# A spectral filter and a mixture of experts in one kernel: the second batch's transform takes one product instead of two from its sixth step on

## The chip, the cores and the metric

The kernel runs on one core of one Trainium2 chip. A core has five engines that work at the same time and wait for each other by semaphores: PE (TensorE, matrix products; its weight loads are listed as PEld), DVE (VectorE), ACT (ScalarE), POOL (GpSimd) and SP (SyncE, which here issues most transfers). Each works through its own list of instructions strictly in order. The metric is the device time of one execution in microseconds (us).

## The reference

Eight batches of 2496 tokens with 256 channels are filtered along the tokens by a Fourier transform, and each filtered token then goes through one of eight experts, the one that its own routing logits choose:

```python
X = np.fft.rfft(x, axis=1)
F = (filt_r + 1j * filt_i)[None, :, :]
y = np.fft.irfft(X * F, n=x.shape[1], axis=1)      # per batch
...
logits = xn @ en.T / tau                            # xn, en: rows of unit length
expert_idx = np.argmax(logits, axis=1)
probs = softmax(logits)                             # written out in the reference
for e in range(E):
    h = np.maximum(x[mask] @ w1[e], 0.0)
    out[mask] = gate_w[mask, None] * (h @ w2[e])
```

In the second half `x` is the filtered signal, `gate_w` the probability of the chosen expert, and `mask` the tokens that chose expert `e`.

## The kernel before

**The filter.** 2496 is 64 times 39, so the transform of a batch is done in two directions: along b (39 long) and along a (64 long). Each batch is a group `g`, 0 to 7, and goes through three parts. `conv_s1` (L448) transforms along b and writes to DRAM (`SD`). `conv_s2` (L469) reads that back in ten steps, and in each step transforms along a, multiplies by the filter and transforms back along a, and writes to DRAM (`ZD`). `conv_sb` (L562) reads `ZD`, transforms back along b (tiles `y`), makes the rows of the tokens, their logits and their place in the list of their expert, and POOL scatters the rows to DRAM (`XS`) by indirect DMAs.

**One step of `conv_s2`.** PE makes `s2` (shown as `s_g_k`: group, step; `conv_s1`'s tiles `s1` are shown in the same form) from the input `a` and the constant c2: the upper 64 partitions hold the real parts, the lower 64 the imaginary ones. A complex product by the filter needs the spectrum times the real part of the filter (`yy`, DVE, L497) and the spectrum with its halves swapped times the imaginary part (`xs`, DVE, L499, with the sign `sgn`). There are two ways to join them. In groups 0 and 1 (`g < FOLDED`) the halves are not swapped: `xs` is taken from `s2` as it is, and PE makes two products into one tile `sa`, `yy` with m1 and `xs` with m2, whose halves stand swapped (L555). In later groups ACT copies the halves of `s2` crosswise into `xs` (L528, L529), DVE multiplies in place, POOL adds `xs` to `yy` (L536; for the first three steps of the third batch DVE does), and PE makes one product. Two steps later (`SAL`) `sa` of step k follows, ACT copies it to `z` (L558), and a DMA on SP's queue writes it to `ZD`.

**The precision of these products.** In groups 0 to 2 the products of L439 and L555 have f32 operands; a 128x512 product of that kind appears in the trace as two matmul instructions. Products of L444 take three passes over rounded parts.

**The experts.** Tokens are worked off in slots, 128 or 256 rows of one expert (`Slot`, L899). A slot reads its rows from `XS` (`xT`), and for each quarter of F PE makes `ph` (up, L967), ACT and DVE make `h`, and PE makes `po` (down, L992) two quarters later. ACT copies the result to `o` (L1006), and POOL scatters it to the output (L1007). The first eight slots have a fixed expert and 128 rows each (tiles `ph_4_0` and the like, with `xTf`); then come the slots of group 0, and so on, so that the names `ph_0_0` start again with each group.

**The order of the work.** Slots of one group and the filter of the next are interleaved: `spread` takes steps of `later(g)` between the quarters of the slots at a pace worked out from the number of steps and of slots, and where the queue of slots is empty it first takes the next group's filter to its end. The first part of the program, up to the first steps of the fixed slots, stands on PE, ACT, DVE and SP in the order of the code (`manual_schedule`); from there on a scheduler orders the instructions of each engine by its own estimate of when they are ready. So an edit can move other instructions too.

**Buffers.** `s2` and `sa` share two PSUM buffers (`ps_c`), `yy` and `xs` six buffers of SBUF (`hl`, `XYB`), and the inputs `a` and the next batch's `in` four (`INB`).

## Time and profile before

| | us |
|---|---|
| median of three runs (lowest to highest) | 1345.94 (1344.21 to 1347.41) |
| the profiled execution | 1342.77 |
| its span, first to last instruction | 1340.7 |
| PE busy | 1247.3 |
| DVE busy | 941.0 |
| ACT busy | 761.6 |
| POOL busy | 486.0 |

The profile is of one execution. The busy time of an engine says how much it has to do, not what it waits for; the chain of waits follows the work that ended last back from releaser to releaser, and the timelines show, in brackets, how long an engine stood idle before an instruction and what ended that. Times in the rows are from the start of the span. The stretch that the change touches directly, the second batch's `conv_s2` from its sixth step on, lies at about 196 to 225 us. The granted clock (PEclk) is a share of PE's full speed: 1.00 is 2.4 GHz, and stretches at 1.2 GHz lower the mean of a window.

### The profile page before, as it was taken

What the parts mean: (1) busy time and instruction counts of PE and PEld (TensorE: products, weight loads), DVE (VectorE), ACT (ScalarE), POOL (GpSimd) and SP (SyncE); (2) the same over time, 40 slices, a digit from 0 to 9 for tenths busy, and PEclk for the clock granted to TensorE, in tenths of its full rate; (3) what the DMA queues carried; (4) which work ended last, traced back from release to release, by engine and by line L of the source; (5) the groups of instructions that cost most, each with busy time, mean ns of one, the idle gap of its engine ahead of it and who ended that gap; (6) DMA issues with size and microseconds to landing.
All of it is one profiled execution on the core that took longest, in us unless ns stands there. A gap on an engine that the chain in (4) does not pass through costs nothing.

```text
span 1340.7 us, 36475 instructions
## 1 busy us (share of the span) xinstructions
PE 1247.3 (93%) x11027; PEld 979.1 (73%) x11027; DVE 941.0 (70%) x3081; ACT 761.6 (57%) x1760; POOL 486.0 (36%) x566
## 2 busy tenths in 40 slices
PE   7966799978998989999999999999998999999997
PEld 2343586645676768787888788878887888889887
DVE  1446696775688668877888788868785885444664
ACT  2165465845655676668666775778565842333343
POOL 0003312174156325542565256424632165111221
PEclk8988899979999989999999999999999999999999
DMA  7799967988878787769779977787774554221211
GB/s 222 268 310 347 258 186 206 215 244 239 193 187 224 211 182 175 221 191 217 159 196 235 192 191 204 219 186 186 172 205 127 119 119 103 58 49 41 57 42 41
DMA packets 272354, 241.27 MB, mean 180 GB/s; under 512 B 167123, under 2 KB 212182, under 8 KB 270373
## 3 DMA queue, kind: packets, MB, share of 16 engines
q1 hardware_dynamic: 243965, 177.87, 53.0%
q0 software_dynamic: 24320, 57.97, 14.4%
q10 hardware_dynamic: 3880, 3.03, 0.8%
q8 instruction: 104, 1.70, 0.5%
q14 instruction: 85, 0.70, 0.2%
HBM read 122.32 MB, written 85.57 MB: 155 GB/s over the span
## 4 chain that ended last, share of the span: by engine, by line
PE 71%; DMA 17%; DVE 5%; issue 3%; ACT 2%; SPq 1%; POOL 1%; DVEq 0%; ACTq 0%; POOLq 0%
PE ph L967 26%; PE po L992 26%; PE s L444 5%; DMA yT<-rows 4%; DMA f<-ZD 4%; PE s L439 3%; DMA f<-in_filt 3%; PE y L444 3%; PE sa L444 2%; DMA SD<-s 2%; PE sa L555 2%; PE y L439 2%; DMA XS<-rows,ixi 1%; PE tp L593 1%; PE lp L610 1%
## 5 line engine op out<-in xcount | busy, mean ns | idle before, releaser
L992 PE MATMUL po<-W,h 128*128 (+1 forms) x3824 | 494.0, 273 | 0.3 <-DVE h L976 0.3
L967 PE MATMUL ph<-xT,wp 128*128 128x256 f16 (+2 forms) x4224 | 472.3, 258 | 9.0 <-DMA xT<-XS 3.9
L967 PEld LDWEIGHTS <-wp 128*128 128x128 f16 x4224 | 358.0, 98 | 85.8 <-issue 37.0
L992 PEld LDWEIGHTS <-h 128*128 128x128 f16 x3824 | 360.9, 98 | 69.7 <-issue 25.9
L975 ACT ACTIVATE h<-ph 128x512 f16<-128x512 f32 (+2 forms) x384 | 202.0, 527 | 246.8 <-PE ph L967 194.1
L1007 POOL DMA_INDIRECT out_dram<-o,meta x153 | 158.7, 1037 | 330.7 <-ACT o L1006 250.6
L976 DVE SCALAR_TENSOR_TENSOR h<-ph,h 128x512 f16<-128x512 f32 (+2 forms) x384 | 227.4, 592 | 46.0 <-ACT h L975 44.1
L951 DVE COPY wp<-W 128x1024 f16 x352 | 166.4, 473 | 120.2 <-PE ph L967 117.0
L790 POOL DMA_INDIRECT XS<-rows,ixi x176 | 179.9, 1022 | 128.6 <-issue 97.1
L536 POOL TENSOR_TENSOR yy<-yy,xs 128x512 f32<-128x512 f32 x57 | 77.6, 1364 | 98.9 <-DVE xs L499 72.3
L497 DVE TENSOR_TENSOR yy<-s,f 128x256 f32<-128x256 f32 x160 | 61.5, 417 | 56.3 <-DMA f<-in_filt 22.9
L400 POOL DMA_DIRECT2D in<-in_x x66 | 38.9, 590 | 160.5 <-DVE xp L413 53.9
L635 DVE SCALAR_TENSOR_TENSOR rows<-y,rr,rows 128x256 f16<-128x256 f32 x176 | 76.7, 477 | 23.6 <-ACT rows L632 22.1
L668 ACT ACTIVATE rows<-y 128x256 f16<-128x256 f32 x176 | 67.1, 396 | 28.8 <-PE y L439 27.4
L632 ACT ACTIVATE rows<-y,rr 128x256 f16<-128x256 f32 x176 | 75.4, 493 | 10.3 <-DVE rr L673 8.3
L1006 ACT ACTIVATE o<-po,meta 128x256 f32<-128x256 f32 x148 | 64.0, 479 | 28.9 <-PE po L992 27.5
L558 ACT COPY z<-sa 128x512 f32<-128x512 f32 x80 | 46.7, 584 | 43.9 <-PE sa L555 37.6
L465 ACT COPY s<-s 128x512 f32<-128x512 f32 x88 | 52.4, 596 | 26.3 <-PE s L439 17.7
L412 ACT CAST yp<-yy 128x512 fp32r<-128x512 f32 x50 | 31.0, 619 | 62.3 <-POOL yy L536 62.0
L595 ACT COPY yT<-tp 128x512 f16<-128x512 f16 x99 | 58.5, 604 | 12.8 <-PE tp L593 8.4
L444 PE MATMUL s<-xp,c1h 117*128 117x512 f32 (+1 forms) x144 | 61.3, 432 | 0.0
L499 DVE SCALAR_TENSOR_TENSOR xs<-xs,sgn_sb,f 128x256 f32<-128x256 f32 x120 | 58.8, 529 | 0.0
(209 smaller groups left out, 1659.1 us busy)
## 6 DMA issues: line engine op xcount, KB each, us to landing
f<-in_filt SPq DMA_DIRECT2D x160, 256.0 KB
a<-SD SPq DMA_DIRECT2D x80, 256.0 KB
ZD<-z SPq DMA_DIRECT2D x80, 256.0 KB
f<-ZD SPq DMA_DIRECT2D x80, 240.0 KB
SD<-s SPq DMA_DIRECT2D x70, 240.0 KB
in<-in_x POOLq DMA_DIRECT2D x66, 234.0 KB
W<-in_w SPq DMA_DIRECT2D x14, 1024.0 KB
in<-in_x SPq DMA_DIRECT2D x22, 234.0 KB
```

What stands on the lines that cost most here:

```text
L444: nc.tensor.matmul(out_, w[:k], b, start=(n == 0), stop=(n == 2))
L536: (nc.vector if g == 2 and k < 3 else nc.gpsimd).tensor_tensor(out=yy, in0=yy, in1=xs, op=ALU.add)
L632: nc.scalar.activation(rows[:, i, 0:D], y[:, i], AF.Copy, scale=rr[:, u:u + 1])
L635: nc.vector.scalar_tensor_tensor(out=rows[:, i, D:2 * D], in0=y[:, i], scalar=rr[:, u:u + 1], in1=rows[:, i, 0:D], op0=ALU.mult, op1=ALU.s ...
L668: nc.scalar.activation(rows[:, i, D:2 * D], y[:, i], AF.Square, accum_out=ssq[:, u + i:u + i + 1])
L790: i = nc.gpsimd.indirect_dma_start(out=XS, out_offset=bass.IndirectOffsetOnAxis(ap=ix, axis=0), in_=src, in_offset=None)
L951: last["dve"] = nc.vector.tensor_copy(wp, src)
L967: last["pe"] = nc.tensor.matmul(ph[:, fi, :size], wp[:, k * 2 + wh, fi * P:(fi + 1) * P], xT[:, xh * 2 + k, :size], start=(c == 0), stop=( ...
L975: last["act"] = nc.scalar.activation(h[:, 0, :, :size], ph[:, :, :size], AF.Relu)
L976: last["lo"] = nc.vector.scalar_tensor_tensor(out=h[:, 1, :, :size], in0=ph[:, :, :size], scalar=0.0, in1=h[:, 0, :, :size], op0=ALU.max, ...
L992: nc.tensor.matmul(self.po[:, s], h, self.Wp[:, off + wh * 1024:off + wh * 1024 + D], start=(fp == 0 and fi == 0 and c == 0), stop=(fp == ...
L1007: i = nc.gpsimd.indirect_dma_start(out=out, out_offset=bass.IndirectOffsetOnAxis(ap=self.meta[:n, s, 0:1].bitcast(I32), axis=0), in_=o, in ...
```

## The change

`FOLDED` no longer counts groups but steps of group 1: group 0 takes two products as before, groups 2 to 7 one as before, and group 1 two up to its fifth step and one from its sixth on (k = 5 to 9).

```diff
--- before.py
+++ after.py
@@ -62,7 +62,7 @@
 WARM = {-1: 8, 12: 26, 35: 22, 40: 6}
 FRONT = 0
 FIXED = 128
-FOLDED = 2
+FOLDED = 5
 PT = 1
 
 
@@ -515,6 +515,7 @@
         for k in range(NK + lag):
             if k + INB - 1 < NK:
                 ain[k + INB - 1] = load_a(k + INB - 1)
+            swap = g > 1 or g == 1 and k >= FOLDED
             if k < NK:
                 pt = ps_c.tile([P, 2, D], F32, tag="c", name=f"s2_{g}_{k}")
                 if g >= G_S2:
@@ -524,15 +525,15 @@
                 product(pt.rearrange("p j c -> p (j c)"), cons["c2"], ain.pop(k))
 
                 xs = cw.tile([P, 2, D], F32, tag="hl", bufs=XYB, name=f"xs{g}_{k}")
-                if g >= FOLDED:
+                if swap:
                     nc.scalar.copy(xs[0:NA], pt[NA:P])
                     nc.scalar.copy(xs[NA:P], pt[0:NA])
                 fts = fin.pop(k)
                 yy = cw.tile([P, 2, D], F32, tag="hl", bufs=XYB, name=f"yy{g}_{k}")
                 filtered(yy, pt, fts, 0)
-                filtered(xs, xs if g >= FOLDED else pt, fts, 1)
+                filtered(xs, xs if swap else pt, fts, 1)
                 ys[k] = [yy]
-                if g >= FOLDED:
+                if swap:
                     (nc.vector if g == 2 and k < 3 else nc.gpsimd).tensor_tensor(out=yy, in0=yy, in1=xs, op=ALU.add)
                 else:
```

For each of these five steps there are two more ACT copies and one POOL addition, and one product less; the DVE multiplication of `xs` reads `xs` where it read `s2`. From L515 on, lines stand one further down in the changed kernel.

The order of other instructions changes as well, from the second batch's sixth step to the third batch's end; on each engine it is the same again from the first steps of the fourth batch's `conv_s2` on. Three places follow; "..." stands for rows left out, most of them repeats with their weight loads.

On PE, at the last two steps of the second batch's `conv_s2` (`sa_8`, `sa_9`), among the last fixed slots (`ph_7`, `po_6`, `po_7`); `s_2_0` is the first product of the third batch's `conv_s1`. Before:

```order
L555 MATMUL sa_8_2450<-yy_8_2394,m_sb 128x512
L555 MATMUL sa_8_2450<-xs_8_2393,m_sb 128x512
L932 TENSOR_LOAD tb_2017
...
L967 MATMUL ph_7_1_2793<-xTf_2074,W 128x128
...
L992 MATMUL po_6_2638<-W,h_6_3_2675 128x256
...
L555 MATMUL sa_9_2474<-yy_9_2432,m_sb 128x512
L555 MATMUL sa_9_2474<-xs_9_2431,m_sb 128x512
...
L967 MATMUL ph_7_2_2910<-xTf_2074,W 128x128
```

And now:

```order
L556 MATMUL sa_8_2462<-yy_8_2404,m_sb 128x512
...
L968 MATMUL ph_7_2_2920<-xTf_2074,W 128x128
...
L993 MATMUL po_7_2951<-W,h_7_0_2746 128x256
...
L993 MATMUL po_7_2951<-W,h_7_1_2847 128x256
...
L968 MATMUL ph_7_3_2990<-xTf_2074,W 128x128
...
L993 MATMUL po_7_2951<-W,h_7_2_2933 128x256
L556 MATMUL sa_9_2485<-yy_9_2444,m_sb 128x512
L444 MATMUL s_2_0_2579<-xp_0_0_2575,c1h 128x512
L444 MATMUL s_2_0_2579<-xp_0_0_2575,c1l 128x512
L444 MATMUL s_2_0_2579<-xp_0_1_2576,c1h 128x512
```

`sa_9` now has the slot products `ph_7_2`, `ph_7_3` and 13 of `po_7` ahead of it, and the product of `xs` is gone.

On POOL, first around the additions of the last two steps, then where the second batch's rows are scattered (L790 before, L791 now; `o_3` is the result of group 0's fourth slot). Before:

```order
L400 DMA in_3_2563<-in_x 117x512
L400 DMA in_4_2625<-in_x 117x512
L400 DMA in_5_2680<-in_x 117x512
L400 DMA in_6_2739<-in_x 117x512
L1007 DMA out_dram<-o_6_0_2874,metaf_2075 19968x256
...
L1007 DMA out_dram<-o_2_0_4135,meta_2_3584 19968x256
L790 DMA XS<-rows_4_2784,ixi_4_3487 161920x258 x2
L790 DMA XS<-rows_5_2887,ixi_4_3487 161920x258 x2
L790 DMA XS<-rows_6_2956,ixi_4_3487 161920x258 x2
L790 DMA XS<-rows_7_3042,ixi_4_3487 161920x258 x2
L1007 DMA out_dram<-o_3_0_4337,meta_3_3835 19968x256
L790 DMA XS<-rows_8_3153,ixi_8_3665 161920x258 x2
```

And now:

```order
L400 DMA in_3_2573<-in_x 117x512
L537 TENSOR_TENSOR yy_8_2404<-yy_8_2404,xs_8_2401 128x512
L1008 DMA out_dram<-o_6_0_2884,metaf_2075 19968x256
L537 TENSOR_TENSOR yy_9_2444<-yy_9_2444,xs_9_2441 128x512
L400 DMA in_4_2635<-in_x 117x512
...
L1008 DMA out_dram<-o_2_0_4145,meta_2_3594 19968x256
L1008 DMA out_dram<-o_3_0_4347,meta_3_3845 19968x256
L791 DMA XS<-rows_4_2794,ixi_4_3497 161920x258 x2
L791 DMA XS<-rows_5_2897,ixi_4_3497 161920x258 x2
L791 DMA XS<-rows_6_2966,ixi_4_3497 161920x258 x2
L791 DMA XS<-rows_7_3052,ixi_4_3497 161920x258 x2
L791 DMA XS<-rows_8_3163,ixi_8_3675 161920x258 x2
```

The addition for `yy_9` stands behind the output of `o_6`, and the output of `o_3` has moved from between the second and third block of scatters to in front of the second.

On PE, where the second batch's first slot (`ph_0_0`) comes among the steps of the third batch's `conv_s2` (`s_2_k` from `a_k`, `sa_k`). Before:

```order
L555 MATMUL sa_2_4025<-yy_2_3947,m_sb 128x512
L439 MATMUL s_2_5_4038<-a_5_3940,c_sb 128x512
L555 MATMUL sa_3_4053<-yy_3_3975,m_sb 128x512
L439 MATMUL s_2_6_4109<-a_6_3968,c_sb 128x512
L555 MATMUL sa_4_4124<-yy_4_4015,m_sb 128x512
...
L967 MATMUL ph_0_0_4249<-xT_0_4096,wp_0_0_4213 128x256
...
L967 MATMUL ph_0_1_4278<-xT_0_4096,wp_0_1_4247 128x256
...
L439 MATMUL s_2_7_4140<-a_7_4008,c_sb 128x512
...
L555 MATMUL sa_5_4155<-yy_5_4043,m_sb 128x512
```

And now:

```order
L439 MATMUL s_2_5_4048<-a_5_3950,c_sb 128x512
L556 MATMUL sa_3_4063<-yy_3_3985,m_sb 128x512
...
L968 MATMUL ph_0_0_4259<-xT_0_4106,wp_0_0_4223 128x256
...
L968 MATMUL ph_0_1_4288<-xT_0_4106,wp_0_1_4257 128x256
...
L439 MATMUL s_2_6_4119<-a_6_3978,c_sb 128x512
...
L556 MATMUL sa_4_4134<-yy_4_4025,m_sb 128x512
```

The slot's first products stand in front of `s_2_6` and `sa_4` instead of behind them.

## Rows read from the trace of the kernel before

**Rows 1.** The page: the span, and PE's busy time, share and instructions.

```profile
span 1340.7 us, 36475 instructions
...
PE 1247.3 (93%) x11027; PEld 979.1 (73%) x11027; DVE 941.0 (70%) x3081; ACT 761.6 (57%) x1760; POOL 486.0 (36%) x566
```

**Rows 2.** Busy time by windows: us, each engine (instructions), PE clock, DMA.

```profile
core 0: us, PE busy (x) PEld busy (x) DVE busy (x) ACT busy (x) POOL busy (x), PEclk, DMA share, GB/s
200.00:210.00 10.00, 10.00 (x70) 6.06 (x69) 8.41 (x27) 4.58 (x10) 2.83 (x3) 1.00 0.71 205
210.00:220.00 10.00, 10.00 (x80) 6.69 (x78) 9.51 (x22) 6.54 (x15) 2.24 (x3) 1.00 0.62 222
...
340.00:350.00 10.00, 8.38 (x46) 5.40 (x47) 4.41 (x13) 4.76 (x16) 0.00 (x0) 0.83 0.90 176
...
370.00:380.00 10.00, 10.00 (x97) 7.61 (x95) 8.93 (x47) 8.62 (x27) 6.17 (x7) 1.00 0.84 198
```

**Rows 3.** The chain of waits, 194 to 240 us: start, us, what.

```profile
205.34 0.67 PE ph L967 x12
...
222.58 1.72 PE sa L555 x4
...
228.77 6.66 DMA f<-ZD
```

**Rows 4.** PE's timeline: start us, us, instruction, count, idle before it and its releaser.

```profile
223.28 1.02 PE L555 MATMUL sa<-xs,m_sb 128*128 128x512 f32 x2
...
233.17 1.13 PE L439 MATMUL y<-f,csb_sb 120*128 120x512 f32 x2 [1.70 <-DMA f<-ZD]
...
308.90 2.34 PE L967 MATMUL ph<-xT,wp 128*128 128x256 f16 x20 [2.43 <-DMA xT<-XS]
...
341.62 1.93 PE L439 MATMUL y<-f,csb_sb 120*128 120x512 f32 x2 [3.28 <-DMA f<-ZD]
...
419.31 2.25 PE L967 MATMUL ph<-xT,wp 128*128 128x256 f16 x19 [1.46 <-DMA xT<-XS]
```

**Rows 5.** The chain of waits, 280 to 345 us.

```profile
299.65 5.90 DMA XS<-rows,ixi
...
319.26 1.31 PE ph L967 x12
...
330.54 0.59 ACT z L558
...
331.15 2.84 DMA ZD<-z
...
334.13 7.45 DMA f<-ZD
```

**Rows 6.** Groups by line: engine, operation, count, ns shortest/median/longest, first and last start.

```profile
L528 ACT COPY xs<-s x60: 582/582/587, 283.8 to 1017.2; 64x512 f32<-64x512 f32 x60
...
L529 ACT COPY xs<-s x60: 577/577/581, 284.4 to 1017.8; 64x512 f32<-64x512 f32 x60
...
L536 POOL TENSOR_TENSOR yy<-yy,xs x57: 1260/1293/1916, 300.6 to 1020.1; 128x512 f32<-128x512 f32 x57
```

**Rows 7.** DVE's timeline, 295 to 330 us.

```profile
300.57 1.94 DVE L499 SCALAR_TENSOR_TENSOR xs<-xs,sgn_sb,f 128x256 f32<-128x256 f32 x2
...
305.14 0.87 DVE L499 SCALAR_TENSOR_TENSOR xs<-xs,sgn_sb,f 128x256 f32<-128x256 f32 x2
...
326.17 1.76 DVE L413 TENSOR_TENSOR xp<-in,xp 117x512 fp32r<-117x512 f32 x1
...
328.52 0.67 DVE L413 TENSOR_TENSOR xp<-in,xp 117x512 fp32r<-117x512 f32 x1
```

**Rows 8.** POOL's timeline, 285 to 330 us.

```profile
291.37 1.16 POOL L1007 DMA_INDIRECT out_dram<-o,meta  x1 [0.30 <-issue]
292.84 1.28 POOL L790 DMA_INDIRECT XS<-rows,ixi  x1 [0.30 <-DVE us L864]
...
300.56 1.26 POOL L536 TENSOR_TENSOR yy<-yy,xs 128x512 f32<-128x512 f32 x1
...
326.09 1.29 POOL L536 TENSOR_TENSOR yy<-yy,xs 128x512 f32<-128x512 f32 x1 [2.00 <-DVE xs L499]
```

## The prediction

> **What bounds the kernel now.** I read the page first: TensorE (PE) is busy 93% of the span [rows 1], so any PE instruction taken away looks like time gained. Then the windows, for the stretch in which the second batch goes through its transform along a. From 200 to 220 us PE is busy 20 of 20 us at full granted clock, and VectorE (DVE) 8.41 and 9.51 of 10 [rows 2]: PE is full and DVE nearly so. Then the chain of waits. To the last product of the transform the chain is PE without a gap; right behind it stands a transfer of 6.66 us, the read of f from ZD [rows 3]. On PE's timeline the last product issues from 223.28 and is over at about 224.1 (0.86 later); the first product that needs that transfer, y_0 of the second batch, starts at 233.17 after 1.70 us of idle PE [rows 4]. So the stretch has two clocks: PE's work in its written order, and the path of the batch: sa_9, copy, write to ZD, read back, y. PE waits for the path, not the path for PE.
>
> The same picture comes twice more. The second batch's rows are scattered from POOL one after the other, the last at 299.65; its landing, 5.90 us, holds the read of the first slot [rows 5], and PE takes that slot up at 308.90 after 2.43 us of idling [rows 4]. And in the third batch the copy behind its last product starts at 330.54, the write takes 2.84 and the read 7.45 us [rows 5], and PE stands idle for 3.28 us before y_0 at 341.62 [rows 4].
>
> **What goes.** Five products of xs with m2. A pair of products (yy and xs) takes 1.72 us on PE [rows 3], one of them 0.86, so 5 x 0.86 = 4.3 us leave PE while it is full. DVE keeps its four multiplications a step; the one for xs reads SBUF instead of PSUM.
>
> **What comes.** Ten ACT copies of 0.58 us and five POOL adds of 1.26 to 1.9, median 1.29 [rows 6]. ACT gets 5.8 us in 25; it lies beside PE. For the last step it is a path: copies 0.58 + 0.58, xs on DVE 0.87 [rows 7], add 1.26 [rows 8], 3.3 us in sum. In front of yy_9's add POOL has the DMA of o_6 (second order excerpt), 1.16 us and 0.30 of issue for such a one [rows 8]: 4.8 us. Between s_1_9 and sa_9 PE has by the new order 36 products of 128 columns, 19 of 256 and two of the f32 kind (sa_7, sa_8): at 0.67 and 1.31 us per 12 [rows 3, 5] that is 2.0 + 2.1 + 1.7 = 5.8 us. The cover is 1.0 us, and one queueing of DVE behind an add uses it up. I take 0.3 us late; the ends are 0 and 3.3 (the second rival).
>
> **What moves.** The order is rebuilt from 195 us until the third batch is through; from the fourth batch's transform on it is the same as before. So a shift at that point goes to the end unchanged, and I follow the path to there.
>
> 1. sa_9 of the second batch. Ahead of it now stand 24 slot products of 128 columns and 16 of 256 that stood behind it (first excerpt): 1.3 + 1.7 = 3.1 us. Of the 4.3 us, 1.2 are left to the path; less 0.3 for the add, 0.9.
> 2. y_0 of the second batch. Between sa_9 and it the order has 8 products of 128 columns and 11 of 256 fewer, 0.4 + 1.2 us; with the 1.2 of point 1 PE's work ahead of it falls by 2.8 to 2.9, while its data comes 0.9 earlier: the idle time of 1.70 becomes about 3.7. After an idle time of 3.28 the next pair took 1.93 us at a granted clock of 0.83, after 1.70 it took 1.13 [rows 2, 4]; for that I charge 0.5 of the 0.8. Path: 0.4 us earlier.
> 3. The scatter. The DMA of o_3, 1.16 us and its issue of 0.30 between the second and third block of scatters [rows 8], now stands in front of the second block (second excerpt), where POOL waits for the indices anyway. Path: 1.9 us earlier, first slot at about 307.0.
> 4. The third batch's transform. Before, s_2_6 and sa_4 stood ahead of the first slot; now behind (third excerpt), and 25 more slot products stand among its steps. From that slot to the end of sa_9 it was 120 products of 256 columns and 8 f32 ones, 13.1 + 6.9 = 20.0 us (21.4 on the clock, 308.90 to 330.3); it becomes 145 and 10, 15.8 + 8.6 = 24.4. That is 4.4 us, and sa_9 and y_0 come 4.4 - 1.9 = 2.5 us later than now.
> 5. Up to the first slot PE's work falls by 6.0 us (the 4.3, and s_2_6 and sa_4 with 1.7), to sa_9 it rises by the 4.4, to y_0 it falls by 0.4; of the 4.3 in all, 4.3 - 6.0 + 4.4 - 0.4 = 2.3 are left to fall behind y_0, up to where both orders agree; by the count there 2.2. PE is full there (10.00 of 10 in 370 to 380) [rows 2], so it counts: 2.5 - 2.2 = 0.3 us later.
>
> Sum: 4.3 us leave PE, and all of it is handed back as idle time in front of transfers. The profiled execution took 1342.77 us (its span is 1340.7) [rows 1]; it becomes 1343.0. The median of the three runs, 1345.94, lies 3.2 higher, so I forecast 1346.0 for the median.
>
> **A rule against the change.** With an add at 300.56, the two xs of DVE that start at 300.57 took 1.94 us, otherwise 0.87; with an add at 326.09 an xp at 326.17 took 1.76, otherwise 0.67 [rows 7, 8]. So the instruction that starts second loses about 1.08 us. The Trainium skill's page "SBUF — State Buffer", section "Who interferes with whom", states that VectorE instructions with two SBUF inputs and a GpSimd instruction that reads SBUF take one port in turn, the second blocking fully. By that rule, the trace agrees, and each add can hold DVE for nearly its length; xs from SBUF and the weights' L331 in this stretch have two SBUF inputs. Without the rule five adds would cost DVE nothing.
>
> **Rivals.** *It stays gained.* If PE's order and not the path set the end, the 4.3 us stay, with the 1.5 of the scatter 5.8: 1337.0 to 1338.5 profiled, 1340.1 to 1341.6 on the median. The same comes if in the third batch the reads of the filter and not PE's order set sa_9, for then the 4.4 of point 4 fall away: 1342.8 + 0.3 - 4.4 = 1338.7. For it: PE without a gap from 200 to 220 [rows 2]. Against: the three idle times at 233, 308 and 341 [rows 4].
> *DVE is held by the adds: slower.* Place: 200 to 222 us. DVE has 20.0 - 17.9 = 2.1 us free there [rows 2]. Five adds at 1.08 take 5.4; 3.3 are over, and they fall on yy_9 and so on sa_9, whose 0.3 become 3.3: 1346.0 profiled, 1349.1 on the median. It decides from about four adds of five that meet a two-input DVE instruction. For it: the two pairs of rows above. Against: of 57 adds the median is 1.29 with a shortest of 1.26 [rows 6], so most meet nothing, and behind 220 DVE has room.
> *It does not do what it says:* the order has five m2 products fewer and five adds more, so this I leave out.
>
> **How the numbers follow.** This kernel's runs tell 0.2% (2.7 us) from no change. Forecast, within that: 0.49. Gained for good: 0.29. DVE held, or point 4 larger than counted: 0.22. The forecast's own spread is some 2 us each way for a transfer that meets others, and 1.5 for the runs. For 8 in 10 the range takes in most of the first rival (1340.5) and the second with its runs' spread (1350.0).
>
> **What would show it.** Products of sa from xs fall from 40 instructions to 30, copies and adds rise by 10 and 5. Point 1: sa_9 ends 0 to 1.5 us before 224.1. Point 2: the wait before y_0 grows from 1.70 to over 3. Point 3: no DMA of o between the scatters, first slot near 307. Point 4: third batch's y_0 near 344 instead of 341.62. Point 5: at the first slot of the third batch's rows, now 419.31 [rows 4], the two traces lie within 2 us. Wrong would be: that slot 4 us earlier (the first rival), or xs and L331 of DVE drawn out beside the adds and sa_9 later than 224.1 (the second).

## The result: slower by 0.8 to 0.9%, where no change was forecast

| | median us (lowest to highest, runs) | ratio to before in the same series (95% interval) |
|---|---|---|
| before | 1345.94 (1340.63 to 1347.48, 5) | |
| changed | 1354.65 (1352.18 to 1359.40, 5) | 1.0081 (1.0053 to 1.0110) |
| changed, once more | 1350.25 (1342.35 to 1356.08, 6) | 1.0094 (1.0057 to 1.0131) |

The forecast was 1346.0, and its range ended at 1350.0. The profiled execution took 1355.93 us.

In two of the series below (e5 to e8, g1 to g4) every kernel took 8 to 10% longer, the kernel before too (1479.82 and 1470.86 us), so that their totals are compared only within a series, and otherwise only distances in the trace's first 240 us are read from them.

### The profile page after: what moved, and what is told of

Same layout as the page of the kernel before. It is cut to its first block, busy times and chain, and to the rows that moved or that the text cites. A ratio compares the mean times of both kernels' runs of the same rounds, so it can differ in the third digit from the quotient of the medians.

```text
span 1354.1 us, 36481 instructions
## 1 busy us (share of the span) xinstructions
PE 1256.7 (93%) x11017; PEld 984.2 (73%) x11017; DVE 941.9 (70%) x3081; ACT 766.9 (57%) x1770; POOL 495.0 (37%) x571
## 4 chain that ended last, share of the span: by engine, by line
PE 52%; DMA 9%; issue 3%; DVE 2%; ACT 2%; POOL 1%; SPq 0%; DVEq 0%; POOLq 0%; ACTq 0%
PE ph L968 21%; PE po L993 20%; PE s L444 4%; DMA yT<-rows 3%; PE y L444 2%; PE sa L444 2%; DMA XS<-rows,ixi 2%; DMA f<-ZD 1%; DMA a<-SD 1%; PE tp L594 1%; PE lp L611 1%; DMA f<-in_filt 1%; POOL out_dram L1008 1%; DVE h L977 1%; DVE wp L952 0%
## 5 line engine op out<-in xcount | busy, mean ns | idle before, releaser
L791 POOL DMA_INDIRECT XS<-rows,ixi x176 | 181.5, 1031 | 127.8 <-issue 95.1
L537 POOL TENSOR_TENSOR yy<-yy,xs 128x512 f32<-128x512 f32 x62 | 84.1, 1359 | 110.1 <-DVE xs L499 87.2
L611 PEld LDWEIGHTS <-yT 128*128 128x128 f16 x704 | 33.2, 98 | 38.4 <-DMA yT<-rows 20.7
```

The source lines that it names most:

```text
L537: (nc.vector if g == 2 and k < 3 else nc.gpsimd).tensor_tensor(out=yy, in0=yy, in1=xs, op=ALU.add)
L791: i = nc.gpsimd.indirect_dma_start(out=XS, out_offset=bass.IndirectOffsetOnAxis(ap=ix, axis=0), in_=src, in_offset=None)
```

## The profile after

The page of the changed kernel (span, then busy time, share and instructions of each engine), against [rows 1]:

```profile
span 1354.1 us, 36481 instructions
PE 1256.7 (93%) x11017; PEld 984.2 (73%) x11017; DVE 941.9 (70%) x3081; ACT 766.9 (57%) x1770; POOL 495.0 (37%) x571
```

PE is listed as busy for 9.4 us more although five products went. The windows of [rows 2] once more (stretch, length, busy us of PE, PEld, DVE, ACT, POOL, granted clock, share and rate of the DMA engines):

```profile
200.00:210.00 10.00, 10.00 (x83) 6.77 (x82) 9.90 (x22) 6.26 (x13) 5.45 (x5) 1.00 0.77 193
210.00:220.00 10.00, 7.63 (x49) 5.04 (x49) 8.46 (x17) 8.08 (x16) 3.10 (x3) 0.83 0.54 193
340.00:350.00 10.00, 8.95 (x69) 6.83 (x67) 5.83 (x11) 4.55 (x9) 4.35 (x9) 1.00 0.94 214
370.00:380.00 10.00, 9.30 (x83) 6.60 (x82) 7.49 (x33) 8.24 (x26) 0.00 (x0) 1.00 0.87 192
```

And a short stretch of the same view:

```profile
214.00:216.00 2.00, 2.00 (x10) 0.93 (x9) 2.00 (x2) 1.99 (x5) 1.81 (x2) 0.50 0.85 283
```

From 210 to 220, where PE had no gap before, it is now idle for 2.4 us and its mean granted clock is 0.83: part of what follows the gap runs at the lower level (0.50 from 214 to 216). DVE, which had 1.6 us free from 200 to 210, has 0.1. PE's timeline shows what that is worth at the five places of [rows 4] (start, length, what ended the idle time in brackets): the last sa of the second batch, its y_0, the first slot, the third batch's y_0 and its first slot.

```profile
227.24 1.02 PE L556 MATMUL sa<-yy,m_sb 128*128 128x512 f32 x2
...
236.20 1.25 PE L439 MATMUL y<-f,csb_sb 120*128 120x512 f32 x2 [2.47 <-DMA f<-ZD]
...
315.25 1.16 PE L968 MATMUL ph<-xT,wp 128*128 128x256 f16 x6 [3.99 <-DMA xT<-XS]
...
351.82 1.13 PE L439 MATMUL y<-f,csb_sb 120*128 120x512 f32 x2 [2.88 <-DMA f<-ZD]
...
427.21 2.03 PE L968 MATMUL ph<-xT,wp 128*128 128x256 f16 x17 [0.62 <-DMA xT<-XS]
```

Against [rows 4] the last sa starts 4.0 us later, y_0 3.0, the first slot 6.4, the third batch's y_0 10.2, the next batch's first slot 7.9. The loss begins before sa_9. Four engines show how. POOL, the adds of the second batch's steps:

```profile
200.93 1.27 POOL L537 TENSOR_TENSOR yy<-yy,xs 128x512 f32<-128x512 f32 x1 [8.91 <-DVE xs L499]
...
206.48 1.26 POOL L537 TENSOR_TENSOR yy<-yy,xs 128x512 f32<-128x512 f32 x1 [1.72 <-DVE xs L499]
...
214.56 1.28 POOL L537 TENSOR_TENSOR yy<-yy,xs 128x512 f32<-128x512 f32 x1
...
221.10 1.28 POOL L537 TENSOR_TENSOR yy<-yy,xs 128x512 f32<-128x512 f32 x1
...
224.82 1.84 POOL L537 TENSOR_TENSOR yy<-yy,xs 128x512 f32<-128x512 f32 x1
```

DVE beside them:

```profile
201.00 2.28 DVE L331 SCALAR_TENSOR_TENSOR W<-W,wsc 128x1024 f16<-128x1024 f32 x1
203.54 1.27 DVE L331 SCALAR_TENSOR_TENSOR W<-W,wsc 128x1024 f16<-128x1024 f32 x1
...
206.59 1.18 DVE L301 TENSOR_SCALAR wq<-wall 128x2 int32<-128x2 int32 x1
207.80 0.22 DVE L304 TENSOR_SCALAR wsc<-wq 128x1 int32<-128x1 int32 x2
...
211.76 0.76 DVE L497 TENSOR_TENSOR yy<-s,f 128x256 f32<-128x256 f32 x2 [1.54 <-ACT xs L530]
...
213.55 2.85 DVE L331 SCALAR_TENSOR_TENSOR W<-wraw,wsc,W 128x512 f16<-128x512 f32 x2
216.66 1.40 DVE L331 SCALAR_TENSOR_TENSOR W<-wraw,wsc,W 128x512 f16<-128x512 f32 x2
220.44 2.50 DVE L331 SCALAR_TENSOR_TENSOR W<-wraw,wsc,W 128x512 f16<-128x512 f32 x2
```

ACT, from the casts of the weights to the copies of step 7 (L529, L530):

```profile
207.98 2.56 ACT L324 ACTIVATE W<-wraw,wsc 128x512 f16<-128x512 f32 x4 [1.81 <-DVE wsc L304]
210.56 0.58 ACT L529 COPY xs<-s 64x512 f32<-64x512 f32 x1
211.15 0.58 ACT L530 COPY xs<-s 64x512 f32<-64x512 f32 x1
211.75 0.59 ACT L559 COPY z<-sa 128x512 f32<-128x512 f32 x1
```

And PE:

```profile
209.18 0.83 PE L968 MATMUL ph<-xTf,W 128*128 128x128 f16 x12
212.39 1.33 PE L439 MATMUL s<-a,c_sb 128*128 128x512 f32 x2 [2.37 <-ACT z L559]
213.51 1.91 PE L556 MATMUL sa<-yy,m_sb 128*128 128x512 f32 x2
215.22 1.06 PE L968 MATMUL ph<-xTf,W 128*128 128x128 f16 x8
```

Read from top to bottom it is one chain. An add starts at 206.48, and an instruction of two columns that starts 0.11 us behind it on DVE takes 1.18 us instead of the 0.15 that it takes without an add (in the kernel before, shown next, and in f3 below): 1.03 lost. The scale wsc comes late, ACT's four casts wait 1.81 us for it, behind them in ACT's order stand the two copies of step 7, 1.16 us, and behind these the copy z of sa_5. That sa had been issued at 207.11; until z has read it, its PSUM buffer isn't free, and by the releaser that the profile names the next s2 gets that buffer: z ends at 212.34, s2 starts at 212.39 after 2.37 us of idle PE. Of these, 1.03 + 1.16 = 2.2 are, by this count, the add's hold and the two copies. Before, ACT had no more than two casts in a row here, and z waited for nothing but its sa (DVE's and ACT's timelines of the kernel before):

```profile
204.68 0.15 DVE L301 TENSOR_SCALAR wq<-wall 128x2 int32<-128x2 int32 x1
...
207.36 1.33 ACT L324 ACTIVATE W<-wraw,wsc 128x512 f16<-128x512 f32 x2
210.06 0.59 ACT L558 COPY z<-sa 128x512 f32<-128x512 f32 x1 [1.37 <-PE sa L555]
```

In the changed kernel yy of step 7 has waited 1.54 us for the second copy meanwhile, and the first products after the gap run at the lower clock. ([rows 6] holds for the copies' own length: 0.58 us here too.) One chain is not yet the price: f4 below takes sa's buffer out of it, and as much is lost.

## The experiments

Theory A: the copies on ACT come late behind the weights' casts and keep PSUM buffers (the expectations take yy for what comes late then; by the rows above it is z, and sa's buffer). Theory B: the adds on POOL hold DVE or come late. Theory C: the order that the scheduler rebuilt costs PE.

One measure will serve throughout: **D**, the time from the start of the second batch's sa_2 to the start of its last product of sa_9. (sa_0 and sa_1 start at 159.60 and 171.85 us in the kernel before, ahead of all that the change touches; where the expectations write sa_0, they mean the row of sa_2.) In the kernel before these are this row and the 223.28 of [rows 4], D = 28.92 us:

```profile
194.36 1.02 PE L555 MATMUL sa<-yy,m_sb 128*128 128x512 f32 x2
```

The changed kernel has 227.24 - 193.99 = 33.25, and 32.93 in the second trace. Totals of one kernel scatter over 1%; D of the six kernels with two traces agreed within 0.1 us for four and within 0.4 for the others. D holds more than lost time: each edit gives a new order, and some put slot products ahead of sa_9 that stood behind it. These are counted in the traces and priced as in the prediction, at 0.67 us per 12 of 128 columns and 1.31 per 12 of 256.

### One part at a time, in the order that each gets (e1 to e4)

e1, from the changed kernel:

```diff
-                    (nc.vector if g == 2 and k < 3 else nc.gpsimd).tensor_tensor(out=yy, ...
+                    (nc.vector if g == 1 or g == 2 and k < 3 else nc.gpsimd).tensor_tensor(out=yy, ...
```

> The five additions go from POOL to DVE (0.67 us each there); the ten ACT copies and the missing products stay as in the change. Theory A, the ACT copies: they stand behind the casts of the weights on ACT and keep the PSUM buffer of s2, PE stops at s_1_8 as in the change; the time stays 6 to 11 us above before. Theory B, POOL's additions: they hold DVE at the port (the 2-column L301 took 1.18 us instead of 0.15 beside one) and come late themselves; without them the stop of 2.37 us at s_1_8 shrinks under 1 us, sa_9 ends before 226 and the time is within 3 us of before. Theory C, the rebuilt order: the time is not told by either and follows where sa_9, y_0 and the first slot stand.

Measured 1352.97, ratio 1.0072 (1.0035 to 1.0108), D = 30.94. PE's wait of 2.37 is gone (0.66 at most), no DVE instruction is drawn out, and D is 2.3 less than in the changed kernel although this order has 1.3 us more of slot products ahead of sa_9. Theory B has its place for sa_9, but not its time: the kernel is as slow. y_0 starts 42.36 us behind sa_2, as late as in the changed kernel (42.21), after 4.19 us of waiting for the read of f from ZD; why that read lands late was not followed.

e2, from the changed kernel: copies, but no add; PE makes two products again, both with m1.

```diff
-                if swap:
+                if swap and g > 1:
                     (nc.vector if g == 2 and k < 3 else nc.gpsimd).tensor_tensor(out=yy, ...
-                        nc.tensor.matmul(zp, m2_sb if n else cons["m1"], ...
+                        nc.tensor.matmul(zp, m2_sb if n and not (g == 1 and j >= FOLDED) else cons["m1"], ...
```

> From the sixth step on ACT copies the swapped halves as in the change, but nothing is added on POOL: PE makes two products, both with m1. So the copies' cost stands alone, PE's work is that of before. Theory A: slower than before by 5 to 12 us, with PE waiting at s_1_8 for ACT. Theory B: within 3 us of before. Theory C: somewhere between, as the order falls.

Measured 1348.52, 1.0033 (1.0004 to 1.0062), D = 29.86, 0.94 more than before. All of that is order: 11 slot products of 128 columns and 3 of 256 more stand ahead of sa_9 (0.6 + 0.3), and PE is not idle in between. With two products a step, the copies cost nothing at sa_9.

e3, from the kernel before: the product of xs is left out in steps 5 to 9, with nothing in its place.

```diff
-                    ys[k].append(xs)
+                    if g == 0 or k < 5:
+                        ys[k].append(xs)
```

> From the sixth step on of the second batch the product of xs is left out and nothing takes its place (the part of the spectrum that the imaginary filter makes is missing there). PE has 4.3 us less to do, no copy and no addition is added. If PE's work bounded the stretch: 4 us faster. If the path through sa_9, ZD and y bounds it: 0 to 4 us faster, by as much as sa_9 comes earlier. Theory C (the rebuilt order alone costs the time): no gain or slower than before.

Measured 1346.84, 1.0022 (0.9991 to 1.0053), D = 25.02. So 4.3 us of PE's work taken away, at no price, make the kernel no faster. In its trace sa_9 comes 3.9 us sooner than before (by D); the first slot starts at 302.62 after 4.65 us of waiting for xT, 109.94 behind sa_2 where it was 114.54, so that up to there the gain is kept. From there to the third batch's last sa it is 29.67 us, where it was 20.54 before: the new order has 169 slot products of 256 columns there instead of 120. It differs from the order before up to about 550 us, so what e3 shows is the product's absence together with an order.

e4, from the kernel before, two products; POOL multiplies xs by ones, which nothing but sa waits for.

```diff
                     ys[k].append(xs)
+                    if g == 1 and k >= 5:
+                        x4 = xs.rearrange("p j (h c) -> p (j h) c", c=P)
+                        nc.gpsimd.tensor_tensor(out=x4, in0=x4, in1=one16.unsqueeze(1).to_broadcast([P, 4, P]), op=ALU.mult)
```

> As before, with two products, but from the sixth step on POOL multiplies xs by ones in place between DVE and PE: the POOL instruction and its way in front of sa, without copies and without a product less. Theory B: slower than before by 4 us or more, DVE instructions beside these drawn out by about 1 us. Theory A: within 3 us of before.

Measured 1351.70, 1.0051 (1.0016 to 1.0086), but D = 29.47, only 0.55 more, and that is 4 slot products of 128 columns and 3 of 256 in the order. POOL's instructions do draw out DVE here (two pairs of L331 take 2.31 and 2.26 us instead of 1.40), but PE is not idle: with two products a step, its own work covers this too. The loss arises later: a product `rk`, between the second batch's last y and its scatters, starts at 283.39, in the kernel before at 278.23. What causes it there was not followed.

### Buffers of its own for sa (e5, f4)

From the changed kernel. e5 and f4 are the same kernel.

```diff
-                pool, tag = (ps_c, "c") if g else (ps_y, "y")
+                pool, tag = (ps_c, "c") if g and not (g == 1 and j >= FOLDED) else (ps_y, "y")
```

> The changed kernel, with sa of the second batch's last five steps in PSUM buffers of their own, so that s2 no longer waits behind a late yy. Theory A (the ACT copies stand behind the weights' copies, so yy comes late and keeps the PSUM buffer that PE's next s2 needs): the waits of PE around 212 us go from 2.4 to below 0.7, sa_9 ends at 223 to 225.5 instead of 228.3, y_0 of the second batch at 232 to 234; and since the order now has 18.8 us of products between the first slot and the third batch's sa_9 (before 18.8, changed kernel 23.2), median 1342 to 1347. Theory B (the adds on POOL come late or hold DVE, so yy_9 itself is late): sa_9 stays at 227 to 228.5, median 1348 or more. Theory C (PE's rebuilt order costs it): third batch's y_0 back to 340 to 343, median 1342 to 1347 wherever sa_9 stands.

> The kernel of e5_sa_psy again (the changed kernel with sa of the last five steps in PSUM buffers of their own), for the same reason. Theory A (a late yy keeps the buffer of s2): no wait above 0.7 us at 205 to 220 us, sa_9 ends at 223 to 225.5. Theory B (yy_9 itself is late behind copies, multiplications and add): sa_9 at 226 to 228.5. The order has 18.8 us of products between the first slot and the third batch's sa_9, as before; theory C then expects the third batch's y_0 at 340 to 344 and a ratio of 0.999 to 1.004 either way, A and B by themselves one that follows sa_9: below 1.002 at 224, above 1.005 at 228.

Measured 1.0034 (1.0009 to 1.0060) and 1.0093 (1.0055 to 1.0131), median 1353.04. PE's wait of 2.37 becomes two in f4, for yy and for an add, and a third of 1.38 us behind them, for a slot's h from DVE:

```profile
213.78 1.10 PE L439 MATMUL s<-a,c_sb 128*128 128x512 f32 x2 [1.25 <-DVE yy L497]
215.77 1.12 PE L556 MATMUL sa<-yy,m_sb 128*128 128x512 f32 x2 [0.90 <-POOL yy L537]
```

D is 30.28 and 30.18, about 3 us less, but 2.8 of these are slot products that this order has behind sa_9 again. Against e3, which has the same products in D and nothing added, 5.2 us are lost, as much as with the shared buffer (table below). So the buffer is where PE's wait showed, not what the loss hangs on: without it PE waits for yy and the adds themselves, which is nearer to theory B. The time doesn't follow D either: in f4 y_0 starts 43.58 us behind sa_2, in the changed kernel 42.21, because the read of f from ZD lands late (5.41 us of idling in front of y_0). A and C had the time near the kernel before's; both miss it.

### The same change in the first five steps (e6, f1)

```diff
-            swap = g > 1 or g == 1 and k >= FOLDED
+            swap = g > 1 or g == 1 and k < FOLDED
```

> One product in the first five steps of the second batch instead of the last five: as many copies, adds and products saved, at 172 to 197 us instead of 197 to 223. Theory A and B (copies and adds beside the weights' casts are what costs): the same loss of 4 us or more at sa_9 of the second batch (227 to 229 instead of 224.3), median 1349 or more. Theory C (the rebuilt order is what costs): by this order the third batch's sa_9 stands 13.2 us of products behind its first slot instead of 18.8, so that y_0 of the third batch comes 4 to 6 us earlier than before (335.5 to 338), and since the products that stood ahead of it now stand behind it, the median gains less: 1340 to 1345.

> The kernel of e6_first_five again (one product in the second batch's first five steps instead of its last five), since in that series the kernel before took 1480 us and PE stood idle about 1 us before many products with no releaser, which the traces of before and after do not show. Theories A and B (copies and adds beside the weights' casts cost): sa_9 of the second batch at 227 or later, median ratio above 1.003. Theory C (the rebuilt order costs; here it has 13.2 us of products between the first slot and the third batch's sa_9 instead of 18.8): y_0 of the third batch at 334 to 339 instead of 341.6, ratio 0.995 to 1.001.

Measured 0.9843 (0.9786 to 0.9900) and 1.0022 (0.9993 to 1.0051), median 1346.30. It saves the same products and has a better order of the third batch, and f1 gains nothing either: its ratio lies above what theory C expected and below what A and B did. Its D of 27.83 tells little on A and B, since its copies and adds lie mostly ahead of sa_2.

### The third batch's order (e7, e8, f2, f3, h1)

The scheduler gets a priority for the third batch's steps, so that they stand ahead of the slots. e7 and f2 are the changed kernel with it, e8 and f3 are e3 with it; both orders also differ from the unedited ones up to about the fifth batch's first sa.

```diff
         for k in range(NK + lag):
+            with tc.high_priority(offset=150) if g == 2 else ExitStack():
...
             yield W_S2
+            with tc.high_priority(offset=150) if g == 2 else ExitStack():
```

> The changed kernel, with the third batch's transform along a ahead of the slots again in the order (its steps get a higher priority): 16.4 us of products between the first slot and the third batch's sa_9 instead of 23.2 (before 18.8). Up to 300 us the order is that of the changed kernel. Theories A and B (the loss arises at sa_9 of the second batch, 228.3 instead of 224.3, and goes through to the end): third batch's first slot stays at 314 to 316, y_0 of the third batch at 342 to 345, the next batch's first slot still 6 to 8 us later than before (425 to 427), median 1351 or more. Theory C (the rebuilt order costs most of it): the next batch's first slot at 419 to 423, median 1344 to 1349.

> The kernel before without the product of xs in the second batch's steps 5 to 9 (that part of the sum is left out, nothing is put in its place), and with the third batch's transform ahead of the slots in the order. Without the order it took 1346.84 median, none of the 4.3 us of PE being gained. Theory C (the saving is handed back by the rebuilt order): the first slot stays at 302 to 304 and the third batch's y_0 comes at 332 to 336 instead of 342.3, the next batch's first slot 4 to 7 us earlier than before (412 to 415), median 1338 to 1341. Rival (PE is not what sets the end at all, the transfers are, wherever PE's order puts the products): y_0 of the third batch as early, but the next batch's first slot still at 417 to 420 and the median at 1344 to 1348.

> The kernel of e7_order_back again (the changed kernel with the third batch's transform ahead of the slots), for the same reason. Theories A and B (the loss arises before 300 us and stays): the next batch's first slot at 425 to 427, ratio 1.005 or more. Theory C: that slot at 419 to 423, ratio 0.999 to 1.004.

> The kernel of e8_one_product_order_back again (the product of xs left out in steps 5 to 9 of the second batch, the third batch's transform ahead of the slots), for the same reason. Theory C: y_0 of the third batch at 332 to 337, the next batch's first slot at 412 to 416, ratio 0.995 to 0.998 (without the order 1.0022). Rival (transfers set the end, wherever PE's order puts the products): that slot at 417 to 420, ratio 0.999 to 1.003.

Measured: the changed kernel with that order 1.0022 (0.9982 to 1.0062) and 1.0024 (0.9996 to 1.0052), median 1346.25; the kernel with one product and nothing added 0.9907 (0.9863 to 0.9951) and 0.9971 (0.9945 to 0.9998), median 1338.31. Each gains 0.005 to 0.007 on the same kernel without it, which looked like theory C. In front of sa_9 nothing has changed. Changed kernel with the order (f2), sa_2 and sa_9, D = 32.93:

```profile
191.62 1.02 PE L558 MATMUL sa<-yy,m_sb 128*128 128x512 f32 x2
...
224.55 1.02 PE L558 MATMUL sa<-yy,m_sb 128*128 128x512 f32 x2
```

One product and nothing added, with the order (f3), D = 25.02:

```profile
197.89 1.02 PE L558 MATMUL sa<-yy,m_sb 128*128 128x512 f32 x2
...
222.91 1.12 PE L558 MATMUL sa<-yy,m_sb 128*128 128x512 f32 x2
```

The control is the kernel before with the same edit (offset 300; its order differs from before's until some way behind the fifth batch's y_0), run twice:

> The kernel before with only the third batch's transform moved ahead of the slots: 13.7 us of products between the first slot and its sa_9 instead of 18.8, and 3.7 us less ahead of y_0; no product saved, no copy, no add. If f3 owes its gain to the saved products, this one gains at most a third of it: ratio 0.998 to 1.001. If f3 owes it to the order: ratio 0.995 to 0.998, and the next batch's first slot 3 to 6 us earlier.

> The kernel of g4_before_order again (before, with only the third batch's transform moved ahead of the slots), since in that series the kernel before took 1471 us, with PE idle about 1 us before many products without a releaser. If f3 (product left out, order moved: 0.9971) owes its gain to the saved products: ratio 0.998 to 1.001. If it owes it to the order: 0.994 to 0.998, with the third batch's y_0 144 to 147 us after the second batch's sa_0, where it stood 147.3 after it before.

Measured 0.9818 (0.9779 to 0.9857), and 0.9954 (0.9929 to 0.9978), median 1331.47 against 1338.34. That is the version that beats both kernels. It saves no product, and it gains about as much by the order as the changed kernel and e3 do. So theory C falls for the third batch: an earlier transform there is worth some 6 to 9 us to every one of these kernels, and it does not explain why the changed one is slower than the one before. Nor do the totals show the saved product bringing anything on top of it (f3 0.9971, h1 0.9954), though these two orders differ from each other up to about 650 us.

### Which of the two additions (g1 to g3)

All with the third batch's order of f2 and f3. g1 leaves the adds out, g2 the copies, g3 has the adds on DVE (the edit of e1).

```diff
g1:
-                if swap:
+                if swap and g == 1:
+                    pass
+                elif swap:
                     (nc.vector if g == 2 and k < 3 else nc.gpsimd).tensor_tensor(out=yy, ...
g2:
-                if swap:
+                if swap and g > 1:
                     nc.scalar.copy(xs[0:NA], pt[NA:P])
-                filtered(xs, xs if swap else pt, fts, 1)
+                filtered(xs, xs if swap and g > 1 else pt, fts, 1)
```

> Between f3 (neither copies nor adds in the second batch's steps 5 to 9: 0.9971) and f2 (both: 1.0024), with the same third batch's order: the ten ACT copies and the multiplication of xs stay, the POOL adds are left out, so xs is computed and not used. Theory A (the copies stand behind the weights' casts on ACT, yy comes late and keeps s2's PSUM buffer): sa_9 of the second batch 33 to 34 us after its sa_0, as in f2, ratio 1.0015 or more. Theory B (the adds): sa_9 26 to 28 us after sa_0, as in f3, ratio below 0.999.

> The other half: the five POOL adds stay, the ten ACT copies are left out, so xs is added with its halves unswapped. Theory A: sa_9 26 to 28.5 us after sa_0, ratio below 0.999. Theory B: sa_9 32 to 34 us after sa_0, ratio 1.0015 or more. If only both together cost (the chain copies, multiplications, add is too long for the two steps between s2 and sa), this run and the one with the copies alone both lie below 1.000 and their losses over f3 add up to less than f2's 7 us.

> f2 with the five adds on DVE: copies, multiplications and add as in f2, without POOL. If the length of the chain from s2 to sa costs: sa_9 31 to 33 us after sa_0, ratio 1.001 to 1.004, near f2. Theory B (POOL's adds and DVE's instructions hold each other up): ratio 0.996 to 0.999, as f3, since the adds on DVE hold nobody at a port.

| in steps 5 to 9, one product | D, us | loss at sa_9 | of it slot products moved ahead | rest | ratio (e7, e8; g1 to g3) | ratio (f2, f3) |
|---|---|---|---|---|---|---|
| nothing added (e8; f3) | 25.02 | | | | 0.9907 | 0.9971 |
| copies (g1) | 27.01 | 1.99 | 0.7 | 1.3 | 0.9951 (0.9920 to 0.9982) | |
| adds on POOL (g2) | 29.51 | 4.49 | 1.4 | 3.1 | 0.9959 (0.9928 to 0.9990) | |
| copies, adds on DVE (g3) | 30.94 | 5.92 | 4.1 | 1.8 | 0.9994 (0.9959 to 1.0029) | |
| copies, adds on POOL (e7; f2) | 32.93 | 7.91 | 2.8 | 5.2 | 1.0022 | 1.0024 |
| the same, sa with buffers of its own (f4) | 30.18 | 5.16 | 0.0 | 5.2 | | |

The slot products are, in pairs of 128 and 256 columns: g1 12 and 0 more than f3, g2 12 and 7, g3 36 and 19, f2 24 and 13. f4 does not have f2's order of the third batch, but has e3's and f3's slot products in D. The ratios in the column before the last come from two series (e7 and e8; g1 to g3), each against its own runs of before, and the steps are larger there than in the last column (from nothing to both 0.0115 against 0.0053). In that order the ratios rise as D does, but neighbours' intervals overlap.

Copies alone lose 2.0 us, so A by itself is refuted; adds alone 4.5, less than B expected; the two add up to 6.48 of 7.91, as the third case of g2's expectation has it, and both lie below 1.000. Without the moved slot products it is 1.3 and 3.1, 4.4 of 5.2: the adds are the larger part, the copies the smaller, and 0.8 come from the two in a row. g3 has sa_9 where the length of the chain would put it and its ratio between the two ranges, but most of its loss is order: the adds on DVE leave 1.8 us where those on POOL leave 5.2. In g2, without a copy, POOL and DVE show B plainly, an add and the two L331 beside it:

```profile
221.89 1.70 POOL L538 TENSOR_TENSOR yy<-yy,xs 128x512 f32<-128x512 f32 x1 [1.29 <-DVE xs L499]
```

```profile
222.72 2.08 DVE L331 SCALAR_TENSOR_TENSOR W<-wraw,wsc,W 128x512 f16<-128x512 f32 x2
225.06 1.40 DVE L331 SCALAR_TENSOR_TENSOR W<-wraw,wsc,W 128x512 f16<-128x512 f32 x2
```

In f3, without adds, nothing of that kind, and the two-column instruction at its short length:

```profile
208.20 0.15 DVE L301 TENSOR_SCALAR wq<-wall 128x2 int32<-128x2 int32 x1
...
212.81 1.41 DVE L331 SCALAR_TENSOR_TENSOR W<-wraw,wsc,W 128x512 f16<-128x512 f32 x2
```

### The changed kernel once more (h2)

> The changed kernel again, beside the kernel before in one series. Where the loss is of the change and not of one execution: sa_9 34 to 34.5 us after the second batch's sa_0 (before 29.9), y_0 41.5 to 43 (before 38.8), first slot 119 to 123 (before 114.5), third batch's y_0 155 to 158.5 (before 147.3), ratio 1.005 to 1.010. Where a part is that execution's: y_10 77 to 79 us after sa_0 instead of the 82.1 of its first trace (its waits for yT and the half clock behind them were longer than in the other traces), and the distances behind it 3 to 4 us shorter than those.

Ratio 1.0094 (1.0057 to 1.0131). D = 32.93, y_0 41.82 behind sa_2, first slot 118.49, third batch's y_0 156.35: the loss is the change's, and the same wait of 2.37 us stands in the same place. y_10 comes after 78.50 us as expected; the 82.06 of the first trace, and so 3.6 us of its shift, belong to that execution.

## Why the prediction was wrong, step by step

**What bounds the kernel: held for the total.** PE full from 200 to 220 us did not mean that PE's work sets the end. e3 takes the 4.3 us away and puts nothing in their place: 1.0022. But up to the first slot the path did follow PE's work there, 4.6 us sooner; what took the gain back was the third batch's order. And one row was misread: the transfer of 6.66 us in [rows 3] starts at 228.77 and releases the second y, not y_0 at 233.17, and between sa_9 and it the chain has slot products and an xp:

```profile
235.48 1.12 PE L439 MATMUL y<-f,csb_sb 120*128 120x512 f32 x2 [0.41 <-DMA f<-ZD]
```

**What comes: this is the step that failed.** It put the price of ten copies and five adds at 0.3 us, of ends 0 to 3.3, with the words "ACT gets 5.8 us in 25; it lies beside PE" and a cover of 5.8 us for the last step. Measured at sa_9, with copies and adds D is 7.91 us longer (f2 against f3) and 8.23 (the changed kernel's first trace against e3); 2.8 of this are slot products that the new order has ahead of sa_9, and 5.2 and 5.5 are the price. In time it is 0.0053 (f2 and f3) and 0.0059 (changed kernel and e3), 7 to 8 us, each uncertain by 0.004 and with the order's part in it. The forecast missed by 8.65. As a term of point 1, beside its 4.3 and 3.1, the 0.3 would have had to be the same 5.5 (D rose by 4.33; in the second trace by 4.01, and 5.2). Four things were left out. The cover was worked out for the last step alone, where it held (yy_9's add ends at 226.66, sa_9 starts at 227.24), while the loss arises at step 7. ACT's share of time was counted, not its order: the copies stand behind casts that wait for DVE. What stands behind the copies was not named: z, which frees the buffer of the next s2, and yy, which always starts behind the second copy here, so that its 0.74 us belong to the path too. And what goes and what comes were priced apart: with two products a step neither the copies (e2) nor POOL's instructions (e4) make PE wait ahead of sa_9, with one they do (g1, g2). So the product covered them; both together with two products were not run. Of the 8.23, slot products are 2.8, PE's idle times of 2.37 and 0.92 are 3.3, and the remaining 2.2 are products at half clock and idle times too short for the list.

**Point 1 failed with it:** sa_9 0.9 us earlier was predicted; it is 4.0 later. **Point 2 too:** y_0 comes 3.0 us later instead of 0.4 earlier, and its wait is 2.47, not over 3, since now its data and PE's work are late together.

**Point 3 failed in size:** no DMA of o stands between the scatters, as the order says, but from the first `rk` of the last indices to the last scatter the changed kernel needs 20.80 and 20.89 us where it was 21.42: 0.5 to 0.6 earlier, not 1.5; in both traces one of these scatters takes 2.15 us, the others about 1.

**Point 4 held:** from the first slot to the third batch's last sa 25.24 us in both traces, against 20.54; 4.7 where 4.4 was predicted. **Point 5 held:** from the third batch's y_0 to the next batch's first slot 75.39 and 76.20 us against 77.69; 2.3 and 1.5 given back, where 2.2 was predicted. But h1 shows that the kernel before, too, gains by an earlier third batch.

**The rivals.** *It stays gained* is refuted by e3 for the total. *DVE is held by the adds* named the place and the amount: its five adds were to take 5.4 us from DVE. The rows above give 2.28 - 1.27, 1.18 - 0.15, 2.85 - 1.40 and 2.50 - 1.40, and an xp at 225.78 that took 1.42 instead of 0.68: 5.3 us, five adds of five. Its price of 3.3 us at sa_9 was too small for the whole (5.2 to 5.5), since it let the delay reach yy_9 through DVE alone, while PE's longest wait runs through ACT's order. But it is what the adds' place on POOL costs there: with the adds on DVE (g3; e1 has the same D) nothing is drawn out, and 1.8 us are left of 5.2. That it makes up the time is not shown: e1 is not measurably better (1.0072 against 1.0081 and 1.0094).

The Trainium skill's page "SBUF — State Buffer", section "Who interferes with whom", counts beside instructions with two SBUF inputs the tensor_scalar form, in a mode that uses both ports, among those that contend with GpSimd. The trace agrees: L301, with one input, took 1.18 us beside an add in the traces of the changed kernel and of f2 (1.17 in h2), and 0.15 in f3, which has no adds there, and in g2, where none had started. Whether L301 ran in that mode the trace does not tell. The prediction had weighed only the two-input part of that section.

**What stays open.** Every edit gave a new order, so how much of the total is the additions' own and how much the order that came with them is not parted; at sa_9 the table parts them. Between 620 and 632 us, where the orders are alike, the changed kernel loses another 2.8 us on the kernel before's trace. But h2, e1 to e4, f2, f3 and f4 all lose 1.8 to 3.3 us there: it is mostly a wait for yT that was short in the one trace of before. Before, and the changed kernel:

```profile
622.79 0.21 PE L610 MATMUL lp<-ent,yT 128*128 128x16 f16 x2 [1.34 <-DMA yT<-rows]
```

```profile
632.69 0.21 PE L611 MATMUL lp<-ent,yT 128*128 128x16 f16 x2 [3.14 <-DMA yT<-rows]
```

What makes e4 late after sa_9, and why f3's lead over h1 at the fifth batch's first sa (7.0 us, from the second batch's sa_2) is gone at the end, single traces don't tell.

## What to carry to other kernels

An instruction added to an engine with free time is not free: walk that engine's queue at each place where it is added, see what it stands behind, what now waits for it, and which buffer that one was to release. Before you trade work away from the busiest engine, leave the work out with nothing in its place: where even that isn't faster, there is little to trade for. Try what is added with the old work still there, too; here each part alone then cost nothing at sa_9, since the old work covered it. And where totals scatter by 1%, a distance between two instructions on one engine can tell parts apart that the total can't, once the work that the order has put between the two is taken off.

## What the runs showed of the hardware that was not expected

The instruction held longest in proportion was the smallest: two int32 columns on DVE, 0.15 us, took 1.18 beside a POOL add, and ACT (1.81 us), PE (2.37) and DVE itself (1.54) waited in turn for what came of it. And after 2.37 us of idling PE's next f32 product of two instructions started 1.12 us ahead of the one behind it, and that one 1.71 us ahead of the next (212.39, 213.51, 215.22): 1.71 is twice the 0.86 that is half of the pair's 1.72 in [rows 3], and the granted clock from 214 to 216 us is 0.50, the lower of its two levels, 1.2 GHz.
